# Attention and soft-MoE on one core: the side work of the attention loop in another order

## The chip, the cores and the metric

The kernel runs on one core of a Trainium2 chip. The core has a matrix engine (PE, with PEld for its weight loads), a vector engine (DVE), an activation engine (ACT), a general engine (POOL), and a queue engine that starts most transfers here (SP). Each engine runs its own instructions strictly in the order of its queue, and waits on semaphores for the others. The metric is the device time of one execution in microseconds (us); of several executions the median is given.

## The reference

Block-sparse attention over 4 batches, 8 heads, 768 positions and 64 channels is followed by a soft mixture of experts over the 3072 tokens that it gives.

```python
def _attn_ref(q, k, v):                       # block, window = 32, 16
    k_sum = k.reshape(B, H, nb, block, D).max(axis=3)
    v_sum = v.reshape(B, H, nb, block, D).mean(axis=3)
    scores_l = scale * q @ k^T, kept where abs(i - j) < window
    scores_s = scale * q @ k_sum^T + log(block)
    a = softmax over both kinds of keys together
    return a @ concat(v, v_sum)

def _moe_ref(x, phi, w1, w2):                 # 8 experts, 4 slots each
    logits = x @ phi
    d = softmax of logits over the tokens;  slot_input = d.T @ x
    slot_out[e] = relu(slot_input[e] @ w1[e]) @ w2[e]
    c = softmax of logits over the slots;   return c @ slot_out
```

Only the shape of the computation is kept above; everything is float32.

## The kernel before

The attention is a loop of 24 steps (`NSTEP`). A step is one third of the positions (256 of 768, `tp` = 0, 1, 2) of four heads of one batch (`hb`, 0 to 7; three steps in a row share one `hb` and so one tile `kk` of keys and one tile `q`). The loop is a software pipeline written out by hand: in pass `i` stand the scores and the exponentials of step `i`, the transposes of step `a = i-1`, and the product with the values and the normalisation of step `b = i-2`. The order of the instructions in the program is the order on every engine; no scheduler moves anything.

The parts of a step, with their lines before the change:

- `scores` (L226, PE) multiplies q with the keys, into two PSUM tiles `s` that have one buffer each.
- `soft_max` (L245, DVE) adds the mask and finds the row maxima, four for each of two halves, 0 and 1. `soft_exp` of half 0 (L255, ACT) takes four exponentials with the maxima as bias. For half 1, `soft_sub` (L261, POOL) subtracts the maxima, and `soft_exp` (L257, ACT) is one exponential over the whole half.
- `trans` (L267, PE) transposes the exponentials, and `evac` (L272, ACT) copies them to `ptr`.
- `values` (L283, PE) multiplies with v, and `norm` (L301 to L304, DVE) divides by the sums and writes the tokens `x`.
- For the keys of the next `hb`: `k_max` (L179, DVE) reduces blocks of 32 keys, `k_edge` (L195, POOL) and `k_put` (L202, POOL) lay them beside the keys for the scores.
- `put_v` (L339) writes the sums of the blocks of v into the tile of v that `values` reads.

Beside the steps runs side work, in pieces named by a letter and a number. A piece is a generator: `begin` runs it up to its first `yield`, which is its work on PE into a PSUM bank, and `flush` runs the rest, which empties the bank.

- `V n` (`v_sum`, L319): sums of v over blocks for `hb` n, 96 small matmuls into two banks; then four copies on ACT (L330) and four additions on DVE (L332) into `vsst`.
- `X n` (`route_x`, L350): transposes 128 tokens; then a copy on ACT (L353) to `xt`.
- `L n` (`route_l`, L363): the logits of 512 tokens, from four `xt`; then a running maximum on DVE (L381, L382), exponentials and copies on ACT (L383 to L385), and the running sum on DVE (L389).
- `T n` (`route_t`, L395): transposes the exponentials `dt`; then a copy on DVE (L398) to `dsb`.
- `D n` (`route_d`, L406): adds these tokens, weighted, to the slots; then DVE adds the result to `acc` (L421; L419 for the first).

All pieces take their banks in turn from the two of the pool `ps_p`. In the tail every second one comes from `ps_t` (`tail`), which holds the transposes during the loop.

The table `PLAN` says which pieces stand in which pass, to the left of the bar (`front`) or to its right (`back`); `LOADS` says how many pieces of the expert weights (512 KB each) a pass asks for on SP. The list `room` says which buffers a weight piece may take, and from which pass on; the later ones are buffers of the attention that have been used for the last time. On SP a pass also asks for the tile of v eight steps on, and once in three passes for keys and q. After the loop comes a drain with the last routing, then the first expert matmul over 32 weight pieces (L663), the second one (L696), and the combination of the slots, with the output.

Of the kernel before, what the change touches and what calls it, by code (L numbers as in the profile page):

```python
# [21 lines left out]
NSTEP = HB * TPS  # L22
# [16 lines left out]


PLAN = {
    1: "| V0",
    3: "| V1",
    6: "X0 X1 | V2",
    7: "X2 X3 |",
    8: "X4 X5 | L0",
    9: "T0 | V3",
    10: "| D0",
    12: "X6 X7 | V4",
    13: "| L1",  # L50
    14: "T1 | D1",
    15: "X8 X9 | V5",
    16: "X10 X11 |",
    17: "| L2",
    18: "X12 X13 | V6",
    19: "T2 | D2",
    20: "X14 X15 |",
    21: "X16 X17 | V7",
    22: "| L3",
    23: "T3 | D3",  # L60
    24: "X18 X19 |",
}

LOADS = [0, 0, 1, 1, 1, 1, 1, 1, 1, 1, 1, 1, 1, 1, 1, 1, 1, 1, 2, 1, 4, 2, 1, 3, 4, 1]


BESIDE = "C0 C1 S0 C2 S1 C3 S2 C4 S3 C5 S4 S5"
# [7 lines left out]
def attention_soft_moe(  # L75
# [13 lines left out]
    nc = tc.nc  # L89
# [33 lines left out]
    xflat = [x.rearrange("p t c -> p (t c)") for x in xs]  # L123
# [2 lines left out]
    room = [(t, 0) for t in was] + [(vflat[0], 18), (vflat[1], 19), (vflat[2], 20)]  # L126
    room += [(t, 20) for t in kflat[0] + [qflat[0]]] + [(vflat[3], 21), (vflat[4], 22), (vflat[5], 23)]
    room += [(t, 23) for t in kflat[1] + [qflat[1]] + xflat[0:2]] + [(vflat[6], 24), (vflat[7], 25)]
    room += [(t, 26) for t in xflat[2:]]
    NPRE = len(room)  # L130
    slots_ = [t for t, _ in room]
    now = [0]
# [13 lines left out]
    def load_k(hb, pr=None):  # L146
        if hb < HB:
            k = kk[hb % 2][:, K0:EA0]
            c = slice(0, 2 * KP) if pr is None else slice(KP * pr, KP * pr + KP)
            nc.sync.dma_start(out=k[:, c], in_=kx[hb, :, c])  # L150
# [22 lines left out]
    def k_max(hb, part):  # L173
        if hb >= HB:
            return
        if hb not in kst:
            kst[hb] = wk.tile([128, 2, NB], F32, name="ks", bufs=2)
        pr, th = part // 3, part % 3
        nc.vector.reduce_max(  # L179
            out=kst[hb][:, pr, 8 * th : 8 * th + 8],  # L180
            in_=kview(hb)[:, pr, 16 + 256 * th : 272 + 256 * th].rearrange("p (b k) -> p b k", k=32),
            axis=AX,
        )
# [13 lines left out]
    def k_put(hb, eng):  # L197
        if hb >= HB:
            return
        for c in range(2):  # L200
            o = 0 if c else 32
            eng.tensor_copy(  # L202
                out=eview(hb, c)[:, :, :, o : o + NB], in_=kst[hb].unsqueeze(2).broadcast_to([128, 2, NTT, NB])
            )
# [13 lines left out]
    def scores(i):  # L218
        hb, tp = steps[i]
        s = [ps_s.tile([128, 4, 128], F32, name=f"s{r}") for r in range(2)]  # L220
        for u in range(4):
            tt, pr = u // 2, u % 2
            for r in range(2):
                for c in range(2):
                    o = 128 * tt + 64 * c
                    nc.tensor.matmul(  # L226
                        s[r][64 * c : 64 * c + 64, u, :].rearrange("p (a k) -> p a k", a=2),
                        lhsT=qs[hb % NQR][64 * r : 64 * r + 64, tp, pr, o : o + 64],
                        rhs=keys(hb, r, c, pr, 2 * tp + tt),
                        start=True,  # L230
                        stop=True,
                        tile_position=(64 * r, 64 * c),
                    )
        ps_[i] = s

    def soft_max(i, r):
        hb, tp = steps[i]
        s = ps_[i][r]
        m = wk.tile([128, 4], F32, name="m", bufs=4)
        p = wk.tile([128, 4, 128], F32, name="p", bufs=4)  # L240
        for u in range(4):
            t = 2 * tp + u // 2
            mk = 0 if t == 0 else 2 if t == NTT - 1 else 1

            nc.vector.tensor_tensor_reduce(  # L245
                out=p[:, u, :], in0=s[:, u, :], in1=maskv[:, mk, :], scale=-0.125, scalar=-NEG,
                op0=ALU.add, op1=ALU.min, accum_out=m[:, u : u + 1],
            )
        p_[i, r] = p, m
# [9 lines left out]
    def soft_sub(i, r):  # L259
        p, m = p_[i, r]  # L260
        nc.gpsimd.tensor_tensor(out=p, in0=m.unsqueeze(2).broadcast_to([128, 4, 128]), in1=p, op=ALU.subtract)  # L261
# [8 lines left out]
    def evac(i, r):  # L270
        ptr = wk.tile([128, 4, 128], F32, name="ptr", bufs=4)
        nc.scalar.copy(out=ptr, in_=ptr_[i, r])  # L272
        ptr_[i, r] = ptr
# [62 lines left out]
    def put_v(i, c, eng):  # L336
        n0 = 0 if c else 96
        src = vsst[96 : 96 + NB, i // TPS % 2].rearrange("n h c -> n (h c)").unsqueeze(1)
        eng.tensor_copy(  # L339
            out=vs[i % NV][n0 : n0 + NB, c].rearrange("n t h c -> n t (h c)"), in_=src.broadcast_to([NB, 2, 260])  # L340
        )
# [154 lines left out]
    def flush(gs):  # L496
        for g in gs:
            while advance(g):
                pass
# [3 lines left out]
    def begin(names):  # L503
        gs = [pieces_of[n[0]](int(n[1:])) for n in names.split()]
        for g in gs:
            advance(g)
        return gs
# [31 lines left out]


    held = []
    for i in range(NSTEP + 2):
        a, b = i - 1, i - 2
        front, back = (PLAN.get(i, "|")).split("|")
        hb, tp = i // TPS, i % TPS
        now[0] = i
        if i < NSTEP:
            scores(i)
            soft_max(i, 0)
            soft_exp(i, 0)  # L550
            soft_max(i, 1)
            soft_sub(i, 1)
        if tp == 1:
            for part in range(3):
                k_max(hb + 1, part)
            k_edge(hb + 1, nc.gpsimd)
        if tp == 2:
            for part in range(3, 6):
                k_max(hb + 1, part)
            k_put(hb + 1, nc.gpsimd)  # L560
        if 0 <= a < NSTEP:
            trans(a, 0)
            trans(a, 1)
            evac(a, 0)
            evac(a, 1)
        if i < NSTEP:
            soft_exp(i, 1)
        flush(held)
        held = begin(front)
        if b >= 0:  # L570
            values(b)
            norm(b)
        flush(held)
        held = begin(back)
        if i == 1:
            flush(held)
            for c in range(2):
                put_v(0, c, (nc.gpsimd, nc.vector)[c])
        if 0 <= a < NSTEP:
            if i > 1:  # L580
                for c in range(2):
                    put_v(a, c, nc.gpsimd)
        if tp == 0:
            load_k(hb + 1) if hb else None
            load_q(hb + 1) if hb else None
        if b >= 0:
            load_v(b + NV)
        for _ in range(LOADS[i]):
            load_piece()
    flush(held)  # L590

    tail.append(1)
    now[0] = NSTEP + 2
    gx = begin("X20 X21")
    flush(gx)
    gx = begin("X22 X23")
    gl = begin("L4")
    flush(gx)
    flush(gl)
    gt = begin("T4")  # L600
    gl = begin("L5")
    flush(gt)
    flush(gl)
    gd = begin("D4")
    gt = begin("T5")
    flush(gd)
    R = lanes()
    advance(R)
    flush(gt)
# [227 lines left out]
```

## Time and profile before

| what | us |
|---|---|
| median of 3 executions | 267.58 (267.22 to 270.6) |
| the profiled execution | 267.19 |
| its span, first to last instruction | 265.4 |
| PE busy in the span | 193.6 |
| DVE busy | 130.5 |
| ACT busy | 107.9 |
| POOL busy | 75.9 |

The mean granted PE clock was 0.864. The profile of one execution lists for every instruction when it began and how long it took, and infers from semaphore events what each wait ended on. In a row of the timeline the columns are the start in us, the duration in us, engine, line, operation, tiles, and how many instructions are merged; in brackets stands the idle time of that engine just before, and what ended it. In a row of the waits the columns are the engine and the line that waited, the one it waited for, the sum in us, how often, and the longest. The 40 slices of the page (6.6 us each; busy share in tenths, PEclk the granted clock) show the stages at a glance:

```profile
PE   7397667396477848496887476775776899999970
PEclk9659999979769986669797957979599899999996
DMA  7997999527825954284288120941693989999968
```

### The profile page before, as it was taken

What the parts mean: (1) busy time and instruction counts of PE and PEld (TensorE: products, weight loads), DVE (VectorE), ACT (ScalarE), POOL (GpSimd) and SP (SyncE); (2) the same over time, 40 slices, a digit from 0 to 9 for tenths busy, and PEclk for the clock granted to TensorE, in tenths of its full rate; (3) what the DMA queues carried; (4) which work ended last, traced back from release to release, by engine and by line L of the source; (5) the groups of instructions that cost most, each with busy time, mean ns of one, the idle gap of its engine ahead of it and who ended that gap; (6) DMA issues with size and microseconds to landing.
All of it is one profiled execution on the core that took longest, in us unless ns stands there. A gap on an engine that the chain in (4) does not pass through costs nothing.

```text
span 265.4 us, 8592 instructions
## 1 busy us (share of the span) xinstructions
PE 193.6 (73%) x3473; PEld 144.0 (54%) x3473; DVE 130.5 (49%) x671; ACT 107.9 (41%) x277; POOL 75.9 (29%) x139
## 2 busy tenths in 40 slices
PE   7397667396477848496887476775776899999970
PEld 5385556285365646375766345664463455564550
DVE  2658684446248455335482534536333476503470
ACT  1165665536254552245363505555043012302350
POOL 8345555314335441323252404315100100000000
PEclk9659999979769986669797957979599899999996
DMA  7997999527825954284288120941693989999968
GB/s 253 320 318 213 354 269 352 141 60 232 295 109 173 312 153 142 65 318 144 66 261 313 48 81 0 330 170 64 218 415 96 332 290 418 419 416 415 370 256 326
DMA packets 19384, 63.19 MB, mean 238 GB/s; under 512 B 2320, under 2 KB 2320, under 8 KB 19344
## 3 DMA queue, kind: packets, MB, share of 16 engines
q1 hardware_dynamic: 19200, 62.28, 67.0%
q8 instruction: 27, 0.44, 0.6%
q10 hardware_dynamic: 144, 0.36, 0.4%
q14 instruction: 13, 0.11, 0.1%
HBM read 56.34 MB, written 6.29 MB: 236 GB/s over the span
## 4 chain that ended last, share of the span: by engine, by line
PE 52%; DVE 20%; ACT 9%; POOL 8%; issue 6%; DMA 2%; POOLq 0%; SPq 0%; ACTq 0%; DVEq 0%
DVE p L245 12%; PE s L226 12%; POOL p L261 8%; PE o L283 7%; PE hps L663 6%; PE so L696 6%; PE pp L319 4%; ACT p L257 4%; PE pp L406 3%; PE pp L350 3%; PE op L733 3%; PE pt L267 2%; PE pp L363 2%; DVE x L304 2%; ACT xt L353 2%
## 5 line engine op out<-in xcount | busy, mean ns | idle before, releaser
L255 ACT ACTIVATE p<-p,m 128x128 f32<-128x128 f32 x96 | 30.8, 391 | 82.1 <-DVE m L245 82.1
L245 DVE CUSTOM_DVE_ANT_0 p<-s,cs 128x128 f32<-128x128 f32 x192 | 42.5, 287 | 39.2 <-PE s L226 39.2
L261 POOL TENSOR_TENSOR p<-m,p 128x512 f32<-128x512 f32 x24 | 24.9, 1039 | 100.4 <-DVE m L245 100.4
L226 PE MATMUL s<-kk,q 64*64 64x128 f32 x768 | 36.1, 325 | 7.9 <-POOL kk L202 3.7
L283 PE MATMUL o<-v,ptr 120*64 120x65 f32 (+1 forms) x768 | 33.5, 249 | 7.2 <-issue 5.8
L226 PEld LDWEIGHTS s<-kk,q 64*64 64x64 f32 x768 | 28.4, 163 | 16.5 <-issue 7.1
L283 PEld LDWEIGHTS o<-v,ptr 120*64 120x64 f32 (+1 forms) x768 | 29.6, 160 | 11.8 <-issue 10.2
L267 PE MATMUL pt<-ident,p 128*128 128x128 f32 x192 | 31.2, 313 | 1.4 <-issue 1.4
L339 POOL COPY v<-vsst 24x520 f32<-24x520 f32 x47 | 29.1, 620 | 10.6 <-DVE vsst L332 8.3
L267 PEld LDWEIGHTS pt<-ident,p 128*128 128x128 f32 x192 | 24.7, 161 | 8.2 <-issue 7.7
L272 ACT COPY ptr<-pt 128x512 f32<-128x512 f32 x48 | 25.4, 576 | 6.6 <-PE pt L267 6.4
L350 PE MATMUL pp<-ident,x 128*128 128x128 f32 x88 | 14.5, 306 | 12.7 <-ACT vsst L330 7.4
L301 DVE TENSOR_SCALAR z<-o 128x8 f32<-128x8 f32 x24 | 4.0, 165 | 34.3 <-PE o L283 34.1
L350 PEld LDWEIGHTS pp<-ident,x 128*128 128x128 f32 x88 | 11.6, 159 | 14.2 <-ACT vsst L330 7.8
L179 DVE TENSOR_REDUCE ks<-kk 128x8 f32<-128x256 f32 x48 | 17.1, 412 | 4.4 <-DMA kk<-kx 4.3
L257 ACT ACTIVATE p<-p 128x512 f32<-128x512 f32 x24 | 15.1, 630 | 9.8 <-POOL p L261 9.8
L304 DVE TENSOR_TENSOR x<-o,z 128x256 f32<-128x256 f32 x48 | 18.1, 419 | 0.8
L319 PE MATMUL pp<-v,cs 64*32 64x64 f32 x768 | 12.1, 256 | 6.3 <-ACT xt L353 4.0
L245 DVE DVE_READ_ACCUMULATOR2_ANT m<- 128x1 f32 x192 | 16.1, 84 | 0.0
L353 ACT COPY xt<-pp 128x512 f32<-128x512 f32 x22 | 12.1, 582 | 8.8 <-PE pp L350 7.3
L319 PEld LDWEIGHTS pp<-v,cs 64*32 64x32 f32 x768 | 9.7, 120 | 8.4 <-ACT xt L353 5.2
L406 PE MATMUL pp<-x,dsb 128*32 128x512 f32 (+1 forms) x40 | 7.5, 833 | 7.4 <-DVE dsb L398 5.7
(132 smaller groups left out, 220.6 us busy)
## 6 DMA issues: line engine op xcount, KB each, us to landing
wa<-w SPq DMA_DIRECT2D x34, 512.0 KB, 6.7
v<-w SPq DMA_DIRECT2D x12, 512.0 KB, 5.0
kk<-kx SPq DMA_DIRECT2D x7, 800.0 KB, 7.4
q<-qx SPq DMA_DIRECT2D x7, 768.0 KB, 9.3
v<-va SPq DMA_DIRECT2D x24, 195.0 KB, 5.3
v<-vb SPq DMA_DIRECT2D x24, 195.0 KB, 5.5
kk<-w SPq DMA_DIRECT2D x9, 512.0 KB, 6.3
x<-w SPq DMA_DIRECT2D x6, 512.0 KB, 4.7
```

The costliest lines, as they stand in the source:

```text
L226: nc.tensor.matmul(s[r][64 * c : 64 * c + 64, u, :].rearrange("p (a k) -> p a k", a=2), lhsT=qs[hb % NQR][64 * r : 64 * r + 64, tp, pr, o ...
L245: nc.vector.tensor_tensor_reduce(out=p[:, u, :], in0=s[:, u, :], in1=maskv[:, mk, :], scale=-0.125, scalar=-NEG, op0=ALU.add, op1=ALU.min, ...
L255: nc.scalar.activation(out=p[:, u, :], in_=p[:, u, :], func=AF.Exp, scale=-1.0, bias=m[:, u : u + 1])
L257: nc.scalar.activation(out=p, in_=p, func=AF.Exp)
L261: nc.gpsimd.tensor_tensor(out=p, in0=m.unsqueeze(2).broadcast_to([128, 4, 128]), in1=p, op=ALU.subtract)
L267: nc.tensor.transpose(pt[:, u, :], p[:, u, :], ident)
L272: nc.scalar.copy(out=ptr, in_=ptr_[i, r])
L283: nc.tensor.matmul(o[64 * c : 64 * c + 64, r, u, :], lhsT=ptr[0:K, u, 64 * c : 64 * c + 64], rhs=v[0:K, c, tt, 2 * pr + r, :], start=True, ...
L304: nc.vector.tensor_tensor(out=x[:, r], in0=o[:, r, :, 0:64].rearrange("p (t q) d -> p t q d", t=2), in1=z[:, r].rearrange("p (t q) -> p t ...
L319: nc.tensor.matmul(pv[c][32 * g : 32 * g + 32, 0:64], lhsT=cs[64 * c : 64 * c + 64, o : o + 32], rhs=v[64 * c : 64 * c + 64, c, t % 2, g, ...
L339: eng.tensor_copy(out=vs[i % NV][n0 : n0 + NB, c].rearrange("n t h c -> n t (h c)"), in_=src.broadcast_to([NB, 2, 260]))
L350: nc.tensor.transpose(pv[:, 128 * c : 128 * c + 128], x, ident)
```

## The change

The change touches the table `PLAN`, the table `LOADS`, one line of `room`, the body of the loop, and the drain. What each part does:

- V's sums stand one pass earlier (V0 in pass 0 instead of 1, and so on). The rest of the pieces that stood to the right of the bar is flushed at the head of the next pass, before the maxima, and no longer after the last exponential.
- A piece to the left of the bar is begun and flushed at once, between `evac` and the last exponential; before, it was begun there after that exponential and flushed after `norm`.
- The stages of the routing stand a pass apart or more. X20 to X23, L4, L5, T4 and D4, which stood after the loop, stand in passes 24 to 26; the loop has one pass more.
- `put_v` moves to the head of the pass, and so does `k_put`; both are on POOL, ahead of `soft_sub`. The two copies of `put_v` for step 0 are both on POOL (one was on DVE).
- `k_max` stands in `tp` 0 and 1 instead of 1 and 2. The load of keys and q stands in `tp` 2 for `hb`+2, instead of `tp` 0 for `hb`+1: one pass earlier.
- Weight pieces are asked for in other passes, 37 within the loop instead of 34; two of the buffers of `x` are free one pass later.

```diff
@@ PLAN, some lines
-    1: "| V0",
-    6: "X0 X1 | V2",
-    7: "X2 X3 |",
-    8: "X4 X5 | L0",
-    13: "| L1",
-    14: "T1 | D1",
+    0: "| V0",
+    5: "| V2",
+    6: "X0 X1 |",
+    7: "X2 X3 | L0",
+    8: "T0 | V3",
+    12: "X6 X7 | L1",
+    13: "T1 | D1",
+    14: "X8 X9 | V5",
...
+    24: "X18 X19 | L4",
+    25: "T4 ; X20 X21 | D4",
+    26: "X22 X23 | L5",
@@ LOADS
-LOADS = [0, 0, 1, 1, 1, 1, 1, 1, 1, 1, 1, 1, 1, 1, 1, 1, 1, 1, 2, 1, 4, 2, 1, 3, 4, 1]
+LOADS = [0, 1, 1, 1, 1, 1, 1, 1, 1, 1, 1, 1, 1, 1, 1, 1, 1, 1, 1, 1, 5, 1, 1, 7, 1, 1, 2]
@@ the loop
-    for i in range(NSTEP + 2):
+    for i in range(NSTEP + 3):
...
         if i < NSTEP:
             scores(i)
+        if i == NSTEP + 1:
+            tail.append(1)
+        flush(held)
+        if 0 <= a < NSTEP:
+            for c in range(2):
+                put_v(a, c, nc.gpsimd)
+        if tp == 2:
+            k_put(hb + 1, nc.gpsimd)
+        if i < NSTEP:
             soft_max(i, 0)
             soft_exp(i, 0)
             soft_max(i, 1)
             soft_sub(i, 1)
+        if tp < 2:
+            for part in ((0, 1, 2), (3, 4, 5))[tp]:
+                k_max(hb + 1, part)
         if tp == 1:
-            for part in range(3):
-                k_max(hb + 1, part)
             k_edge(hb + 1, nc.gpsimd)
-        if tp == 2:
-            for part in range(3, 6):
-                k_max(hb + 1, part)
-            k_put(hb + 1, nc.gpsimd)
         if 0 <= a < NSTEP:
             trans(a, 0)
             trans(a, 1)
             evac(a, 0)
             evac(a, 1)
+        for group in front.split(";"):
+            flush(begin(group))
         if i < NSTEP:
             soft_exp(i, 1)
-        flush(held)
-        held = begin(front)
-        if b >= 0:
+        if 0 <= b < NSTEP:
             values(b)
             norm(b)
-        flush(held)
         held = begin(back)
...
-        if tp == 0:
-            load_k(hb + 1) if hb else None
-            load_q(hb + 1) if hb else None
+        if tp == 2:
+            load_k(hb + 2)
+            load_q(hb + 2)
         if b >= 0:
             load_v(b + NV)
         for _ in range(LOADS[i]):
             load_piece()
```

In the orders below the changed kernel's lines are one higher than before (L331 is L330 of before). On ACT, in passes 6 to 9 before, from V2's copies (`vsst`) to the first exponentials of L0 (`dt`), with the copies of X2 to X5 (`xt`) between them:

```order
L330 COPY vsst<-pp 24x64 x4
L353 COPY xt<-pp 128x512 x2
L255 ACTIVATE p<-p,m 128x128 x4
L272 COPY ptr<-pt 128x512 x2
L257 ACTIVATE p<-p 128x512
L353 COPY xt<-pp 128x512 x2
L255 ACTIVATE p<-p,m 128x128 x4
L272 COPY ptr<-pt 128x512 x2
L257 ACTIVATE p<-p 128x512
L378 ACTIVATE dt,stat<-pp,stat 128x128
```

The same stretch on ACT after the change, from V2's copies to L0, in passes 6 to 8; the copies of `xt` are X0 to X3:

```order
L331 COPY vsst<-pp 24x64 x4
L256 ACTIVATE p<-p,m 128x128 x4
L273 COPY ptr<-pt 128x512 x2
L354 COPY xt<-pp 128x512 x2
L258 ACTIVATE p<-p 128x512
L256 ACTIVATE p<-p,m 128x128 x4
L273 COPY ptr<-pt 128x512 x2
L354 COPY xt<-pp 128x512 x2
L258 ACTIVATE p<-p 128x512
L379 ACTIVATE dt,stat<-pp,stat 128x128
```

V2's copies moved from behind the last exponential of pass 7 to ahead of the first ones of pass 6; X's copies moved from behind a pass's last exponential to ahead of it; L0's exponentials moved from behind those of pass 9 to ahead of those of pass 8.

On SP, passes 2 and 3 before: tiles of v (`v_93`, `v_94`), the weight pieces (`wa`), and the keys and q of `hb` 2 (`kk_89`, `q_91`):

```order
L159 DMA v_93<-va 96x520
L160 DMA v_93<-vb 96x520
L142 DMA wa_107<-w 128x1024
L150 DMA kk_89<-kx 128x1600
L154 DMA q_91<-qx 128x1536
L159 DMA v_94<-va 96x520
```

The same on SP after the change, from pass 1 on:

```order
L143 DMA wa_107<-w 128x1024
L151 DMA kk_89<-kx 128x1600
L155 DMA q_91<-qx 128x1536
L160 DMA v_93<-va 96x520
L161 DMA v_93<-vb 96x520
L143 DMA wa_108<-w 128x1024
```

The keys moved past a pair of loads of v, and the first weight piece stands ahead of both.

On POOL, passes 4 to 6 before: the subtractions (`p<-m,p`), the edges of the keys, the sums of blocks of v (`v_96`, `v_97`) and of keys (`kk_89<-ks`):

```order
L261 TENSOR_TENSOR p<-m,p 128x512
L195 COPY kk_89<-kk_89 128x12x16 x4
L339 COPY v_96<-vsst 24x520 x2
L261 TENSOR_TENSOR p<-m,p 128x512
L202 COPY kk_89<-ks 128x12x24 x2
L339 COPY v_97<-vsst 24x520 x2
L261 TENSOR_TENSOR p<-m,p 128x512
```

The same on POOL after the change:

```order
L340 COPY v_96<-vsst 24x520 x2
L262 TENSOR_TENSOR p<-m,p 128x512
L196 COPY kk_89<-kk_89 128x12x16 x4
L340 COPY v_97<-vsst 24x520 x2
L203 COPY kk_89<-ks 128x12x24 x2
L262 TENSOR_TENSOR p<-m,p 128x512
```

The copies into v and those of the keys' sums stand ahead of the pass's subtraction now, and behind it before.

More of the change, by code (lines that the diff above doesn't have):

```diff
@@ L41 @@
 PLAN = {
-    1: "| V0",
-    3: "| V1",
-    6: "X0 X1 | V2",
-    7: "X2 X3 |",
-    8: "X4 X5 | L0",
-    9: "T0 | V3",
-    10: "| D0",
-    12: "X6 X7 | V4",
-    13: "| L1",
-    14: "T1 | D1",
[L52 to L61, printed above, removed]
+    0: "| V0",
+    2: "| V1",
+    5: "| V2",
+    6: "X0 X1 |",
+    7: "X2 X3 | L0",
+    8: "T0 | V3",
+    9: "X4 X5 | D0",
+    11: "| V4",
+    12: "X6 X7 | L1",
+    13: "T1 | D1",
+    14: "X8 X9 | V5",
+    15: "X10 X11 | L2",
+    16: "T2 | D2",
+    17: "| V6",
+    18: "X12 X13 |",
+    19: "X14 X15 | L3",
+    20: "T3 | V7",
+    21: "X16 X17 | D3",
+    24: "X18 X19 | L4",
+    25: "T4 ; X20 X21 | D4",
+    26: "X22 X23 | L5",
 }
-LOADS = [0, 0, 1, 1, 1, 1, 1, 1, 1, 1, 1, 1, 1, 1, 1, 1, 1, 1, 2, 1, 4, 2, 1, 3, 4, 1]
+LOADS = [0, 1, 1, 1, 1, 1, 1, 1, 1, 1, 1, 1, 1, 1, 1, 1, 1, 1, 1, 1, 5, 1, 1, 7, 1, 1, 2]
 BESIDE = "C0 C1 S0 C2 S1 C3 S2 C4 S3 C5 S4 S5"
@@ L128, in attention_soft_moe @@
     room += [(t, 23) for t in kflat[1] + [qflat[1]] + xflat[0:2]] + [(vflat[6], 24), (vflat[7], 25)]
-    room += [(t, 26) for t in xflat[2:]]
+    room += [(t, 26) for t in xflat[2:4]] + [(t, 27) for t in xflat[4:]]
     NPRE = len(room)
@@ L565, in attention_soft_moe @@
             evac(a, 1)
+        for group in front.split(";"):
+            flush(begin(group))
         if i < NSTEP:
             soft_exp(i, 1)
-        flush(held)
-        held = begin(front)
-        if b >= 0:
+        if 0 <= b < NSTEP:
             values(b)
             norm(b)
-        flush(held)
         held = begin(back)
[L575 to L582, printed above, removed]
-        if tp == 0:
-            load_k(hb + 1) if hb else None
-            load_q(hb + 1) if hb else None
+        if tp == 2:
+            load_k(hb + 2)
+            load_q(hb + 2)
         if b >= 0:
@@ L590, in attention_soft_moe @@
     flush(held)
[L592 to L604, printed above, removed]
+    now[0] = NSTEP + 3
     gt = begin("T5")
-    flush(gd)
     R = lanes()
```

## The prediction

> **What bounds the kernel now.** I read the stages first (windows: length; busy us and count of PE, PEld, DVE, ACT, POOL; granted clock; DMA share; GB/s), cut where the first masked maximum (L245) of steps 4 and 23 and the first expert matmul (L663, at 209.7) start.
>
> ```profile
> 29.83 0.29 DVE L245 CUSTOM_DVE_ANT_0 p<-s,cs 128x128 f32<-128x128 f32 x1 [1.02 <-PE s L226]
> 181.34 0.29 DVE L245 CUSTOM_DVE_ANT_0 p<-s,cs 128x128 f32<-128x128 f32 x1 [0.65 <-PE s L226]
> ...
> 11.30:29.80 18.50, 15.03 (x412) 12.64 (x411) 12.64 (x83) 11.49 (x30) 9.32 (x15) 0.79 0.93 296
> 29.80:181.30 151.50, 105.75 (x2172) 86.12 (x2172) 77.73 (x457) 71.58 (x190) 54.39 (x93) 0.84 0.56 187
> 181.30:209.70 28.40, 18.66 (x248) 13.35 (x248) 11.95 (x50) 9.86 (x28) 3.80 (x6) 0.88 0.60 220
> 209.70:265.40 55.70, 46.75 (x600) 26.10 (x600) 23.97 (x73) 13.67 (x28) 0.76 (x1) 0.93 0.92 361
> 23.00:47.50 24.50, 17.86 (x508) 15.07 (x504) 15.73 (x95) 14.24 (x36) 13.37 (x23) 1.00 0.91 300
> 101.80:128.00 26.20, 17.95 (x308) 13.89 (x305) 12.10 (x71) 11.21 (x32) 7.80 (x14) 0.76 0.47 161
> ```
>
> Steps 4 to 22 take 151.5 us, 8.0 each, and in them no engine is full: PE 70%, DVE 51%. So order bounds them. PE's waits say which order; one step, 7, shows it in full.
>
> ```profile
> PE pp L350 <- ACT vsst L330: 7.4, 2, 3.7
> PE pp L395 <- ACT dt L383: 6.2, 3, 3.1
> PE s L226 <- POOL kk L202: 3.7, 4, 1.7
> ...
> 47.56 1.10 PE L226 MATMUL s<-kk,q 64*64 64x128 f32 x32
> 48.60 1.09 PE L267 MATMUL pt<-ident,p 128*128 128x128 f32 x8
> 48.81 0.29 DVE L245 CUSTOM_DVE_ANT_0 p<-s,cs 128x128 f32<-128x128 f32 x1 [3.74 <-PE s L226]
> 49.15 1.28 ACT L255 ACTIVATE p<-p,m 128x128 f32<-128x128 f32 x4 [3.79 <-DVE m L245]
> 50.33 1.04 ACT L272 COPY ptr<-pt 128x512 f32<-128x512 f32 x2
> 50.51 1.07 DVE L179 TENSOR_REDUCE ks<-kk 128x8 f32<-128x256 f32 x3
> 50.76 1.04 POOL L261 TENSOR_TENSOR p<-m,p 128x512 f32<-128x512 f32 x1 [5.67 <-DVE m L245]
> 51.84 0.63 ACT L257 ACTIVATE p<-p 128x512 f32<-128x512 f32 x1 [0.46 <-POOL p L261]
> 52.49 0.88 ACT L330 COPY vsst<-pp 24x64 f32<-24x64 f32 x4
> 52.72 0.99 DVE L332 TENSOR_TENSOR vsst<-pp,vsst 24x64 f32<-24x64 f32 x4 [1.15 <-ACT vsst L330]
> 53.42 1.97 PE L350 MATMUL pp<-ident,x 128*128 128x128 f32 x8 [3.73 <-ACT vsst L330]
> 53.84 1.29 POOL L339 COPY v<-vsst 24x520 f32<-24x520 f32 x2 [0.89 <-DVE vsst L332]
> 55.32 1.68 PE L283 MATMUL o<-v,ptr 120*64 120x65 f32 x32
> 56.94 1.10 PE L226 MATMUL s<-kk,q 64*64 64x128 f32 x32
> 57.08 0.17 DVE L301 TENSOR_SCALAR z<-o 128x8 f32<-128x8 f32 x1 [3.38 <-PE o L283]
> 57.52 0.76 DVE L304 TENSOR_TENSOR x<-o,z 128x256 f32<-128x256 f32 x2
> ```
>
> V2's matmuls were done before 47.56, but their copies (L330) stand on ACT behind this step's last exp (L257), which waits for POOL's subtraction. Both PSUM banks stay taken, PE stands 3.73 us before X2 (L350), then runs it and the values at half clock (1.97, 1.68). The step costs 9.4.
>
> **The change, part by part.** The arithmetic per step is the same; its place moves. Durations still needed, at full clock:
>
> ```profile
> 27.47 1.18 PE L319 MATMUL pp<-v,cs 64*32 64x64 f32 x96
> 41.68 1.04 PE L350 MATMUL pp<-ident,x 128*128 128x128 f32 x8
> 59.87 1.15 PE L283 MATMUL o<-v,ptr 120*64 120x65 f32 x32
> 61.74 1.05 ACT L353 COPY xt<-pp 128x512 f32<-128x512 f32 x2
> 71.16 0.28 DVE L398 COPY dsb<-pp 128x128 f32<-128x128 f32 x1
> 79.71 1.06 PE L406 MATMUL pp<-x,dsb 128*32 128x512 f32 x8 [1.69 <-ACT vsst L330]
> 199.47 1.08 PE L363 MATMUL pp<-xt,cs 128*32 128x128 f32 x32
> 202.22 0.22 DVE L389 SCALAR_TENSOR_TENSOR stat<-stat,st 128x1 f32<-128x1 f32 x1 [1.06 <-ACT st L384]
> 202.31 1.08 PE L363 MATMUL pp<-xt,cs 128*32 128x128 f32 x32
> ```
>
> I count from one step's first L245 to the next one's. The eight maxima take 1.7 (48.81 to 50.51, where L179 follows), k's reductions 1.07, the norm 1.2 (57.08 to 58.28); scores and transposes follow each other after 1.04 (47.56 to 48.60).
>
> *Evacuations at the head.* V's copies and adds now run under the next scores (1.04 on PE). The last exp ends 3.65 after the first maximum (52.46 less 48.81), so in a step whose only side work is V the copies wait 0.6 and the adds push the maxima by 0.7: 1.04+1.04+1.15+1.18 on PE and 0.6 make 5.0. A step without side work is DVE's: 1.7+1.07+1.2=4.0, or PE's 1.04+1.04+1.15 with a hop, 3.3, where k's reductions are over. L's chain (matmul end 200.55 to L389's end 202.44: 1.9) leads the maxima and puts them 0.7 later than scores would.
>
> *X ahead of the last exp, its copies at once.* X, values and then V or L: L waits for the second X copy. Scores 1.04, to the first exp 0.55, exps 1.28, ptr copies 1.05, xt copies 1.05, hops 0.3, L 1.08: 6.3, with the next step's L chain 7.0. V instead of L: 6.6; D (needs the first copy only) 5.8; X alone hides under DVE: 4.2. The later exp is 1.1 later, which the next transposes see only after a step of 4.2.
>
> *Stages a step apart.* T|D: L chain, maxima, k's reductions, dsb 0.28, D 1.06: 6.1 from scores, 5.5 between maxima. T|V: 5.05.
>
> The sum, steps 4 to 22: plain 4, 10: 8.0; plain 22: 3.3; X alone 6, 18: 8.4; V 5, 11, 17: 15.0; X|L 7, 12, 15, 19: 28.0; T|D 13, 16: 11.0; T|V 8, 20: 10.1; X|D 9, 21: 11.6; X|V 14: 6.6. Together 102. To it I add 7: 0.2 a step for hops that the sum leaves out (the 0.46 before L257 is such a one), and 3 for k, next.
>
> *Loads of k one step earlier on SP, its reductions one step earlier too.*
>
> ```profile
> 31.91 1.07 DVE L179 TENSOR_REDUCE ks<-kk 128x8 f32<-128x256 f32 x3 [0.31 <-DMA kk<-kx]
> DMA to landing us min/median/max: 4.6/7.4/7.7
> ```
>
> The load is issued when the scores of a head pair's last step end; the reductions come that step's length plus 1.9 later, 6.2 where it is short (4.3). Against 4.6 to 7.7 that is nothing to 1.5 a pair; for steps 5, 11 and 17 I take 1 each, nearest the median. In return k_put is finished a step before the scores that need it: the 3.7 of L202 go. At the start nothing is won: k(1), whose landing was covered, now holds DVE in step 0, and k(2) passes one pair of v loads (2 x 195 KB, 1.3 us at 296 GB/s) and lands at 30.6 at the latest instead of 31.9. I take 29, as it is also issued up to 3 earlier, behind its scores and not behind a load; the reduction and the norm follow, and step 4's first maximum comes at 29+1.07+1.2=31.3, 1.5 later than 29.83. The w piece of step 1, the bursts of 5 and 7 at steps 20 and 23 queue on SP behind buffers that are free by then; DMA share after 30 us is 0.56, so they are hidden; if they are not, the expert stage waits for its later pieces: 512 KB at 296 GB/s is 1.8 each, and both ends of the range leave room for one.
>
> *put_v ahead of the subtraction on POOL.* Two copies (53.84 to 55.13 in step 7) now run under the maxima, when POOL waits (5.67 before L261). At nothing if maxima cover them; at most 1.3 a step where V's adds are late, and then the last exp has 0.5 to spare: both ends are in the range.
>
> A rule speaks against this move: by the Trainium skill, "SBUF — State Buffer", "Who interferes with whom", some DVE operations and GpSimd's block each other for a whole instruction. By it, if the maxima took the pair, a copy could end up to 1.7 later, the length of the maxima. The page lets an operation with one SBUF input go free, and the maxima read PSUM and one SBUF operand; no row here shows it, and the sum stays.
>
> *Drain.* From step 23's maximum: last exp 3.65; transposes, their copies and X18/X19's 3.35; L4 1.2; to dt 1.3; T4 0.4; X20/21 1.0; values 1.15; norm 1.4; X22/23 with copies 1.8; L5 1.1; then, as now from L5's end (203.39) to 209.70, 6.3. That is 22.7 against 28.4. The expert stage keeps 55.7: all pieces that it starts on have landed, and its DMA stream (share 0.92) starts with it.
>
> 31.3+102+7+22.7+55.7 = 218.7 of span. The profiled execution took 267.19 with a span of 265.4, so 1.8 lies around it: 220.5. The median of the runs shown is 267.58, 0.4 above: **221 us**.
>
> **The rivals.** *PE stays cold.* In 101.8 to 128 the clock was 0.76 with PE standing behind side work; in 23 to 47.5, where PE is 73% busy with short waits, 1.00. My rows are at full clock. Steps 4 to 22 hold 19x3.3 of scores, transposes and values, six V, nine X pairs, four L and four D: 87 us of PE work; were a third of it at half clock, as 0.84 means now, it would cost up to 28: 249. Against it: the waits that precede the slow stretches are those removed. The Trainium skill ("TensorE: Matmul & The Clock Gate", Part 1, the HAM clock gate) says the same of the cause: an idle window of about 3.4 us halves the clock, a busy one restores it. By that rule the sum stands, and the trace agrees (3.73 idle, then 1.97 for 1.04).
>
> *k paces the steps, and DVE stands with it: the slower end.* k's first reduction blocks norm and the next maxima. The denser steps ask more of DMA (300 GB/s at share 0.91 in 23 to 47.5, as it stands). If k lands 11 us after issue, 4.8 x 6 pairs less the 3 counted: 247. It decides against the kernel only if k needs some 15.5 us: (273-221+3)/6=9.2 beyond 6.2. The longest now is 7.7.
>
> *The waits only change places.* Head evacuations hold the maxima as much as the old ones held PE; then only k_put's 3.7 and the drain's 5.7 are won, less 1.5: 260, or within 2% with a few late pieces.
>
> **How the numbers follow.** My forecast 0.80; cold PE 0.07; k at 11 us 0.05, at 15 us 0.03; waits change places 0.05. The low end is the sum without the 7 and with a drain 2 shorter: 212. The high end takes half the cold cost and 1 us for k in the other three pairs: 221+14+3, 238. What lies beyond is about 2 in 10. Two per cent, about what a measurement of this kernel tells from no change, is 262 to 273: faster 0.92, same 0.05, slower 0.03.
>
> **What would show it.** PE's waits on L330 and L383 ahead of L350 and L395 gone; PEclk near 1 from 30 us to the expert stage; step 23's maximum near 140 instead of 181.34; L663 near 163; L202 gone from the waits of the scores; new, small: L179 behind DMA, maxima behind L332 and L389. It is wrong if L179 waits several us in each pair, if X|L steps stay near 9, or if the expert stage stretches beyond 56 because its pieces land late.

## The result, and the profile after

The changed kernel takes 220.56 us (median of 4 runs, 218.82 to 224.13); the kernel before took 269.09 us beside it (267.22 to 271.01). The ratio is 0.8175, with a 95% interval of 0.805 to 0.830: faster. The forecast was 221. The profiled execution took 219.1 us with a span of 217.3. Some executions of a kernel are a few per cent slower than the rest, so all ratios and intervals here (not the medians) leave these out, and none is given where too few others were left.

The stages, cut at the same events as in the prediction: the first masked maximum of steps 4 and 23 and the first expert matmul. The diff adds one line ahead of the kernel's functions, so L245 is now L246, and the first expert matmul has become L647. First the three events in the timeline, then the windows with the same columns as before:

```profile
29.92 0.28 DVE L246 CUSTOM_DVE_ANT_0 p<-s,cs 128x128 f32<-128x128 f32 x1
...
139.88 0.29 DVE L246 CUSTOM_DVE_ANT_0 p<-s,cs 128x128 f32<-128x128 f32 x1
...
160.29 0.66 PE L647 MATMUL hps<-wa,W1ST 128*32 128x256 f32 x4 [0.54 <-DVE rz L479]
...
29.90:139.90 110.00, 91.11 (x2178) 75.35 (x2179) 76.60 (x457) 70.91 (x190) 54.21 (x93) 0.95 0.80 245
139.90:160.30 20.40, 15.83 (x241) 11.38 (x240) 9.59 (x46) 9.28 (x25) 3.62 (x6) 0.98 0.89 326
160.30:217.30 57.00, 48.14 (x600) 26.50 (x600) 23.96 (x73) 13.67 (x28) 0.72 (x1) 0.92 0.91 354
```

| stage | before | predicted | after |
|---|---|---|---|
| to step 4's first maximum | 29.8 | 31.3 | 29.9 |
| steps 4 to 22 | 151.5 | 102 + 7 | 110.0 |
| drain | 28.4 | 22.7 | 20.4 |
| expert stage | 55.7 | 55.7 | 57.0 |

DVE, ACT and POOL are as busy in the steps as before (DVE 76.6 us against 77.7); what went is idle time, and PE's slow clock (0.95 granted against 0.84; its busy time fell from 105.8 to 91.1). Now PE's largest waits, in the view of waits (total, times, longest):

```profile
PE s L227 <- issue: 7.1, 3, 3.2
PE o L284 <- issue: 4.8, 3, 2.2
PE s L227 <- DVE m L246: 3.1, 2, 2.7
PE pp L407 <- DVE z L302: 2.3, 2, 1.4
PE s L227 <- DVE kk L203: 2.0, 1, 2.0
PE pp L320 <- issue: 1.7, 1, 1.7
```

The waits for V's copies and L's exp ahead of X and T (7.4 and 6.2) are gone from the head of the list. On top stands something that the prediction never spoke of: three lines of "issue", waits that end with nothing that the profile shows, 13.6 us in seven of them. Step 11 has the longest; its timeline:

```profile
67.49 0.34 SPq L151 DMA_DIRECT2D kk<-kx  x1
67.87 0.53 SPq L155 DMA_DIRECT2D q<-qx  x1
67.92 1.15 PE L284 MATMUL o<-v,ptr 120*64 120x65 f32 x32
...
69.00 1.18 PE L320 MATMUL pp<-v,cs 64*32 64x64 f32 x96
...
73.39 1.36 PE L227 MATMUL s<-kk,q 64*64 64x128 f32 x32 [3.21 <-issue]
...
74.69 1.97 PE L268 MATMUL pt<-ident,p 128*128 128x128 f32 x8
```

Values and V run back to back, then PE stands 3.21 us before the scores, whose inputs were there (POOL's copies into `kk`, the last of them, ended at 69.96), and the transposes behind them run at half clock (1.97 for 1.04). The trace's DMA records tell what came just ahead. Queue q8 carries PE's own instructions, 27 packets of 16 KB in the whole execution:

```profile
q8 instruction: 27, 0.44, 0.9%
```

I set each packet beside the place in PE's program where it is first needed. These places lie 256 PE instructions apart (matmuls, weight loads and the semaphore instructions between them; PE's 7055 records make 27.6 such blocks). All seven waits, then six of the blocks without one; the first column is when PE passed the place before, the third how busy the 16 DMA engines were from then until the packet started (worked out from the records):

```
PE passes   packet          DMA busy   PE passes     of it
a place     start   end     between    next place    waiting
 24.37      28.83   30.23    1.0         31.73        0.85
 31.73      35.34   36.55    1.0         37.90        1.73
 37.90      41.75   42.82    1.0         44.09        1.74
 54.42      58.29   59.55    1.0         61.23        2.19
 67.98      71.07   72.02    0.85        73.39        3.21
 91.96      96.97   98.09    0.93        99.66        0.91
107.16     109.98  111.02    0.90       112.50        2.94
 61.23      62.33   63.52    0.29        67.98        none
122.34     122.73  123.75    0.0        128.34       none
128.34     128.41  129.45    0.0        131.63        none
 20.82      21.36   22.55    1.0         24.37        none
 50.19      51.34   52.80    1.0         54.42        none
 73.39      77.67   78.88    1.0         80.53        none
```

In the two rows with idle DMA engines the packet starts within 0.4 us of PE's passing; in the seven with a wait the engines are nearly full and it starts 2.8 to 5.0 later. Full engines make a packet late often and not always: in two of the last three rows it starts 0.5 and 1.2 later. Nor is a late packet enough for a wait: in the last row it comes 4.3 late, and PE, in part at half clock there, takes 7.1 us for the block. PE goes on 1.3 to 1.7 after the packet's end in each of the seven. So, as an estimate from these rows, a block can be run some 2.5 us after it is asked for at best and 5 to 8 in the seven cases, and PE is through with the 256 before it sooner where V's 192, which take 1.2 us, stand among them. The Trainium skill ("Runtime: NRT & Kernel Launch", Instruction fetch mechanics) describes blocks of 16 KiB, 256 instructions, fetched by the sequencer's own DMA queue. The packets here agree. It also calls the cost mostly hidden, which the 13.6 us here contradict.

### The profile page after: what moved, and what is told of

Same layout as the page of the kernel before. It is cut to its first block, busy times and chain, and to the rows that moved or that the text cites. A ratio compares the mean times of both kernels' runs of the same rounds, so it can differ in the third digit from the quotient of the medians.

```text
span 217.3 us, 8616 instructions
## 1 busy us (share of the span) xinstructions
PE 178.3 (82%) x3473; PEld 132.1 (61%) x3473; DVE 128.4 (59%) x670; ACT 107.4 (49%) x277; POOL 76.6 (35%) x140
## 3 DMA queue, kind: packets, MB, share of 16 engines
HBM read 56.34 MB, written 6.29 MB: 288 GB/s over the span
## 4 chain that ended last, share of the span: by engine, by line
PE 53%; DVE 13%; ACT 10%; issue 8%; POOL 7%; DMA 6%; SPq 0%; POOLq 0%; ACTq 0%
PE hps L647 8%; PE so L680 7%; PE s L227 7%; PE pt L268 6%; PE o L284 6%; DVE p L246 5%; DMA kk<-kx 3%; PE op L717 3%; POOL p L262 3%; PE pp L351 3%; PE pp L407 3%; DMA q<-qx 3%; ACT xt L354 3%; ACT ptr L273 2%; PE pp L320 2%
## 5 line engine op out<-in xcount | busy, mean ns | idle before, releaser
L256 ACT ACTIVATE p<-p,m 128x128 f32<-128x128 f32 x96 | 30.7, 390 | 34.7 <-DVE m L246 34.7
L246 DVE CUSTOM_DVE_ANT_0 p<-s,cs 128x128 f32<-128x128 f32 x192 | 42.5, 286 | 8.8 <-PE s L227 8.3
L227 PE MATMUL s<-kk,q 64*64 64x128 f32 x768 | 30.1, 282 | 12.1 <-issue 7.1
L227 PEld LDWEIGHTS s<-kk,q 64*64 64x64 f32 x768 | 23.1, 136 | 19.0 <-issue 13.6
L284 PE MATMUL o<-v,ptr 120*64 120x65 f32 (+1 forms) x768 | 29.8, 232 | 4.8 <-issue 4.8
L284 PEld LDWEIGHTS o<-v,ptr 120*64 120x64 f32 (+1 forms) x768 | 26.0, 144 | 9.5 <-issue 9.2
L268 PE MATMUL pt<-ident,p 128*128 128x128 f32 x192 | 29.9, 300 | 1.1 <-ACT p L258 0.9
L268 PEld LDWEIGHTS pt<-ident,p 128*128 128x128 f32 x192 | 22.6, 151 | 6.7 <-issue 3.2
L258 ACT ACTIVATE p<-p 128x512 f32<-128x512 f32 x24 | 15.3, 639 | 9.0 <-POOL p L262 9.0
L246 DVE DVE_READ_ACCUMULATOR2_ANT m<- 128x1 f32 x192 | 15.9, 83 | 0.0
L351 PE MATMUL pp<-ident,x 128*128 128x128 f32 x88 | 13.1, 296 | 0.0
L320 PE MATMUL pp<-v,cs 64*32 64x64 f32 x768 | 10.5, 235 | 2.3 <-issue 1.7
L333 DVE TENSOR_TENSOR vsst<-pp,vsst 24x64 f32<-24x64 f32 x32 | 7.2, 224 | 7.3 <-ACT vsst L331 6.5
L647 PE MATMUL hps<-wa,W1ST 128*32 128x256 f32 x136 | 10.9, 468 | 0.5 <-DVE rz L479 0.5
```

What stands on the lines that cost most here:

```text
L227: nc.tensor.matmul(s[r][64 * c : 64 * c + 64, u, :].rearrange("p (a k) -> p a k", a=2), lhsT=qs[hb % NQR][64 * r : 64 * r + 64, tp, pr, o ...
L246: nc.vector.tensor_tensor_reduce(out=p[:, u, :], in0=s[:, u, :], in1=maskv[:, mk, :], scale=-0.125, scalar=-NEG, op0=ALU.add, op1=ALU.min, ...
L256: nc.scalar.activation(out=p[:, u, :], in_=p[:, u, :], func=AF.Exp, scale=-1.0, bias=m[:, u : u + 1])
L268: nc.tensor.transpose(pt[:, u, :], p[:, u, :], ident)
L284: nc.tensor.matmul(o[64 * c : 64 * c + 64, r, u, :], lhsT=ptr[0:K, u, 64 * c : 64 * c + 64], rhs=v[0:K, c, tt, 2 * pr + r, :], start=True, ...
L351: nc.tensor.transpose(pv[:, 128 * c : 128 * c + 128], x, ident)
```

## Experiments: one part alone, or one part undone

In the table: the median; the ratio to the kernel before with its 95% interval (– where none is given); then of the profiled execution the first maximum of step 4, steps 4 to 22, the drain, and, as "instr", the sum of PE's waits for instructions ahead of step 23's maximum: idle time above 0.3 us that ends at the first instruction of a block, 1.2 to 1.7 us after its packet, with the weight loads that run meanwhile taken off (so 13.5 for the 13.6 above). I count them by place and packet and not by the label "issue", because the view of waits names the semaphore event that came last. In u_k it shows

```profile
PE s L227 <- DMA v<-vb: 3.0, 1, 3.0
```

although the scores read no v; this wait too stands at the first instruction of a block and ends 1.3 us after its packet (2.3 us of it count).

| kernel | median us | ratio | to step 4 | steps 4–22 | drain | instr |
|---|---|---|---|---|---|---|
| before | 269.1 | 1 | 29.8 | 151.5 | 28.4 | 8.1 |
| changed | 220.6 | 0.818 (0.805–0.830) | 29.9 | 110.0 | 20.4 | 13.5 |
| b_head | 228.9 | 0.857 (0.841–0.873) | 32.1 | 116.4 | 22.4 | 10.0 |
| u_x | 229.7 | 0.858 (0.841–0.876) | 30.4 | 118.3 | 20.4 | 10.8 |
| u_k | 215.3 | 0.806 (0.794–0.819) | 31.5 | 105.4 | 21.3 | 8.1 |
| u_drain | 220.0 | 0.825 (0.814–0.835) | 30.7 | 113.0 | 21.0 | 13.2 |
| u_drain2 | 221.1 | – | 31.4 | 111.1 | 22.0 | 13.8 |
| e_light | 219.3 | 0.819 (0.813–0.825) | 29.8 | 107.2 | 21.3 | 11.7 |
| e_lk | 213.6 | 0.790 (0.782–0.798) | 29.0 | 106.1 | 21.2 | 7.9 |
| e_v2 | 210.3 | 0.774 (0.768–0.780) | 30.6 | 101.3 | 21.5 | 1.5 |
| e_v2k | 210.5 | 0.788 (0.780–0.796) | 27.6 | 102.5 | 20.7 | 1.9 |
| e_v2l | 209.3 | – | 30.9 | 98.8 | 20.7 | 1.5 |
| c_v2lk | 207.8 | 0.779 (0.774–0.785) | 27.7 | 99.6 | 20.7 | 0.0 |
| e_shift | 224.1 | 0.825 (0.818–0.832) | 38.2 | 110.1 | 20.6 | 15.3 |

**b_head: the evacuations at the head, alone, in the kernel before.**

```diff
             scores(i)
+        flush(held)
+        if i < NSTEP:
             soft_max(i, 0)
...
             soft_exp(i, 1)
-        flush(held)
         held = begin(front)
```

> The kernel before with one line moved: the copies, sums and maxima left over from the step behind (V, L, T, D) are evacuated right behind the scores instead of behind the last exp. Theory (these evacuations held the PSUM banks and are most of the gain): the waits of PE on L330 and L383 go, six V steps and four L steps lose about 3 each, 30 of the 48 us: about 238. Rival (the waits only change places, onto the maxima and k): no more than 10 won, 257 or above.

228.9: more than the theory gave. Moving one flush is worth 40 of the 48.5 us; everything else in the change adds 8. PE's waits in this kernel:

```profile
PE pp L319 <- ACT xt L353: 7.3, 10, 1.5
PE pp L406 <- DVE dsb L398: 6.6, 4, 2.2
PE o L283 <- issue: 4.0, 3, 3.0
```

PE no longer waits for V's copies and L's exponentials ahead of X and T. The largest waits left are those for X's and T's own evacuations (L353, L398) behind the last exp, which the rest of the change moves. The clock follows: 0.97 granted in steps 4 to 22 against 0.84.

**u_x: X and T behind the last exp again.**

```diff
-        for group in front.split(";"):
-            flush(begin(group))
         if i < NSTEP:
             soft_exp(i, 1)
+            held = begin(front)
         if 0 <= b < NSTEP:
             values(b)
             norm(b)
+        if i < NSTEP:
+            flush(held)
```

> The changed kernel with one part undone: the X pieces' copies follow the last exp again and not the copies of ptr. Theory: in the five steps with X and then L or V the copies start at the last exp's end, about 1 us later each, and X with D half of that; 3 to 8 us longer, about 225. Rival (X ahead of the last exp carries much of the gain, since PE stands behind the copies): 15 or more, 236 or above.

229.7, between the two, and the intervals of 0.841 to 0.876 and 0.805 to 0.830 do not meet: X and T ahead are worth about 9. My expectation counted only the steps with X; T rides in the same place. With a step named by its pieces left and right of the bar, T|V in step 8 takes 5.92 for 4.93, T|D in 13 and 16 6.33 for 5.23, X|D in 21 6.32 for 5.45: about 1 in most steps with front work. The waits name both:

```profile
PE pp L407 <- DVE dsb L399: 4.8, 3, 2.4
PE pp L364 <- ACT xt L354: 4.0, 3, 1.4
```

**u_k: k's reductions, copies and loads where they stood.**

```diff
-        if tp == 2:
-            k_put(hb + 1, nc.gpsimd)
...
-        if tp < 2:
-            for part in ((0, 1, 2), (3, 4, 5))[tp]:
-                k_max(hb + 1, part)
         if tp == 1:
+            for part in range(3):
+                k_max(hb + 1, part)
             k_edge(hb + 1, nc.gpsimd)
+        if tp == 2:
+            for part in range(3, 6):
+                k_max(hb + 1, part)
+            k_put(hb + 1, nc.gpsimd)
...
-        if tp == 2:
-            load_k(hb + 2)
-            load_q(hb + 2)
+        if tp == 0 and hb:
+            load_k(hb + 1)
+            load_q(hb + 1)
```

> The changed kernel with one part undone: k's reductions, POOL's edge and block copies and the loads of k and q for the next head pair stand where they stood before. Theory: the scores of a pair's first step wait for POOL's block copies again (3.7 in all before, up to 1.7 a pair where the step is short), 4 to 8 us longer: 225 to 229. Rival (k costs the changed kernel as much as it won, as the 3 us counted for it say): within 2 us of 220.6.

Neither: 215.3, so undoing this part seems to win (the intervals overlap). In the profiled executions the waits for instructions fell from 13.5 to 8.1. The changed kernel issues k and q, 800 and 768 KB a pair, at the end of the steps in which six of the eight V pieces start (2, 5, 8, 11, 14, 17), as in step 11 above. Whether the gain lies in these waits is what e_lk and e_v2k ask below.

**u_drain, u_drain2: the last routing stages after the loop again.** X20 to X23, L4, L5, T4 and D4 go back from PLAN's rows 24 to 26 into the hand-written sequence behind the loop. u_drain leaves out the addition of D4 to `acc`; u_drain2 has it.

```diff
-    24: "X18 X19 | L4",
-    25: "T4 ; X20 X21 | D4",
-    26: "X22 X23 | L5",
+    24: "X18 X19 |",
...
-    for i in range(NSTEP + 3):
+    for i in range(NSTEP + 2):
```

> The changed kernel with one part undone: X20 to X23, L4, L5, T4 and D4 follow the loop one after another again. Theory: the drain from step 23's first maximum to the first expert matmul goes from 20.7 back to about 28.4, the steps stay: 227 to 229. Rival (the drain became shorter only because the steps ahead of it left less behind): 221 to 223.

> The changed kernel with X20 to X23, L4, L5, T4 and D4 after the loop as before, with all of its sums (u_drain leaves out the addition of D4 to the sums in acc). Theory, after u_drain: the drain of about 20 us is not due to these pieces' places, 219 to 222, and the drain from step 23's first maximum to the first expert matmul is within 2 us of 20.7. Rival (the new places save 5 or more in the drain): 225 or above.

220.0 and 221.1, with drains of 21.0 and 22.0 against 20.4: these places are worth at most 1.6 us. b_head's drain of 22.4 tells where most of the 8 came from: the moved flush, which stands in the last passes too.

## Experiments: the waits for instructions

**e_light: fewer transfers early.**

```diff
-LOADS = [0, 1, 1, 1, 1, 1, 1, 1, 1, 1, 1, 1, 1, 1, 1, 1, 1, 1, 1, 1, 5, 1, 1, 7, 1, 1, 2]
+LOADS = [0, 0, 0, 0, 0, 0, 0, 0, 0, 0, 0, 0, 2, 2, 2, 2, 2, 2, 3, 4, 5, 1, 1, 7, 1, 1, 2]
```

> The changed kernel with its weight pieces at other steps: none in steps 0 to 11, two a step in 12 to 17, three and four in 18 and 19, the rest as it was. The changed kernel stood 10 us in steps 3 to 11 where PE waits for nothing but its own instructions; each of these waits ends 1.3 to 1.7 us after a 16 KB packet of the instruction queue has landed, and the packet starts up to 5 us after PE has crossed the place in its program that asks for it. Theory A (the packet queues behind the data transfers): in steps 3 to 11 the packets start within 1 us and the waits fall from 10 to under 3; in 12 to 19 they stay or grow. Rival B (V's 192 instructions in 1.2 us outrun the packets whatever the transfers do): the same waits at the same places, 8 us or more in steps 3 to 11. The whole: 214 to 219 by A, 220 to 222 by B.

Between the two. In steps 3 to 11 the waits are 0.5, 1.35, 0.96 and 3.15 (step 11), 6.0 together at places where there were 9.7. Packets still start up to 4 us late there, since k, q and v are loading too, so A's "within 1 us" and "under 3" fail; B's "8 or more" fails as well. In 12 to 19 there are 5.7, where there were 3.8. The time, 219.3, is hardly less: weight pieces are only a part of what the packets wait behind.

**e_v2: the same block sums in half the matmuls.**

```diff
-                for g in range(4):
+            for g in range(2):
+                for c in range(2):
...
-                        pv[c][32 * g : 32 * g + 32, 0:64],
+                        pv[c][r : r + 32, 0:128].rearrange("p (h d) -> p h d", h=2),
...
-                        rhs=v[64 * c : 64 * c + 64, c, t % 2, g, 0:64],
+                        rhs=v[64 * c : 64 * c + 64, c, t % 2, 2 * g : 2 * g + 2, 0:64],
```

> The changed kernel with V's block sums in 24 matmuls of 128 columns instead of 48 of 64, its copies and sums two each instead of four; the same sums. PE then runs 96 instructions fewer in each of eight V pieces, for 0.4 us more each. By theory B the waits for instructions go nearly all (13.6 to under 4) and the time falls to about 213; by A they fall by less than half, since the packets start as late as before, and the time is 216 to 221.

210.3, better than B's 213. Of the 13.5 us of waits 1.5 are left, and the instruction packets fall from 27 to 24, as 8 x 96 instructions in blocks of 256 should:

```profile
37.19 1.51 PE L321 MATMUL pp<-v,cs 64*32 64x128 f32 x48
...
q8 instruction: 24, 0.39, 0.8%
```

V takes 1.51 now instead of 1.18 and still the steps are 8.7 shorter. Packets still come late: one asked for at 74.28 starts at 79.63, and PE does not wait for it. So both halves are needed for a wait: a late packet (A) and 256 instructions in a hurry (B). Removing the hurry is the one that pays. The edit also halves V's copies and additions, and no run has that alone. Steps 8, 17 and 20, which had no wait for instructions, are 0.3 shorter each (step 17: 4.62 for 4.93); six such steps make some 2 of the 10 us, by estimate.

**e_lk, e_v2k, e_v2l, c_v2lk: the edits combined.** e_lk is e_light with u_k's edit; e_v2k and e_v2l are e_v2 with u_k's edit and with e_light's LOADS; c_v2lk has all three.

> e_light with k's reductions, POOL's edge and block copies and the loads of k and q where they stood before, as in u_k. u_k was 5 us faster than the changed kernel. Theory A (its gain is that the transfers fall at other times against the instruction packets): with the transfers light, e_lk and e_light differ by less than 2 us. Rival (k's new place itself costs about 5): e_lk is 4 us or more under e_light.

> e_v2 with k's reductions, POOL's copies and the loads of k and q where they stood before (the edit of u_k). In e_v2 only 1.5 us of waits for instructions are left, so that k's place shows alone. Theory (u_k won its 5 us because its transfers met the instruction packets at other times; taken without these waits its profiled span is 5 us above the changed kernel's): e_v2k is within 2 us of e_v2's 210.3, or up to 5 slower. Rival (k's new place itself costs about 5): 206 or below.

> e_v2 with the weight pieces at the steps of e_light. With the waits for instructions gone already, theory says that the light steps win nothing more there: within 2 us of 210.3; at most 1 us from a faster start. Rival (the light steps win by themselves, since loads of k and v land sooner): 207 or below.

> All three edits together: V in half the matmuls, light first steps, k at its place of before. If the three were independent gains (10, 1 and 5 us): about 205. By the theory (all three shorten the same waits for instructions, which V's edit removes alone): 208 to 212.

e_lk contradicts theory A as I had put it: k's place won 5.7 although the early transfers were lighter. They were not light enough to test it, as e_light showed (7.9 us of waits are left against 11.7). With V's instructions halved k's place wins nothing: 210.5 against 210.3, and by the ratio it rather loses. If its new place cost 5 us by itself, it would do so there too. So its cost in the changed kernel lies, as far as these runs tell, in the waits for instructions, though e_lk's 5.7 is more than the 3.8 by which its waits fell. (The 5 us between the spans in e_v2k's expectation do not come out of the two profiles: 214.1 less 8.1 is 206.0 for u_k, 217.3 less 13.5 is 203.8 for the changed kernel, 2.2 apart.) Why the old place makes fewer of them stays open: that k and q are issued where V starts fits step 11 of the changed kernel, but u_k still waits 2.3 there, and e_lk 4.4 in step 18. The light steps are worth 1 more, within what the runs can tell. c_v2lk is the lowest median, 207.8, at the lower edge of the theory's 208 to 212, with no wait for instructions above 0.3 us, and 12.8 below the changed kernel; by the ratio (0.774 and 0.779) it is not told from e_v2, so V's edit is what carries it. Both beat the changed kernel. c_v2lk's steps 4 to 22, drain and expert stage:

```profile
27.67:127.27 99.60, 90.29 (x1894) 73.36 (x1893) 74.88 (x447) 68.99 (x179) 54.45 (x94) 1.00 0.84 283
127.27:147.94 20.67, 15.91 (x239) 11.38 (x238) 9.69 (x46) 9.40 (x25) 3.62 (x6) 1.00 0.85 323
147.94:204.46 56.52, 46.81 (x600) 26.07 (x600) 24.08 (x73) 13.67 (x28) 0.74 (x1) 0.92 0.91 357
```

The clock is 1.00 throughout the steps, PE is 91% busy, and the DMA share is not lower than in the changed kernel (0.84 against 0.80): it was not the amount of the transfers that held the steps up.

**e_shift: the same program, its blocks cut elsewhere.**

```diff
+    for _ in range(32):
+        nc.tensor.matmul(wm[:, 0:8], lhsT=acc[:, 0:128], rhs=acc[:, 0:8], start=True, stop=True)
     load_k(0, 0)
```

> The changed kernel with 32 more warm-up matmuls of 8 columns ahead of the loop, 128 PE instructions with their weight loads, in a stretch where PE waits for the first data. Nothing in the loop differs; only where the program's blocks of 256 instructions begin. Theory (one packet carries 256 instructions; a wait arises where PE runs through 256 faster than a packet asked for at their start arrives, 3.5 to 6 us): the waits move. Worked out from the changed kernel's trace with its waits taken out, the fastest blocks end after 2.5 us at V2's matmuls (step 5) and after 2.1 us at the scores behind V3 (about 55 us), so waits of 1 to 4 us come there; the blocks that ended at the scores of steps 11 and 18 (3.2 and 2.9 us of wait) now end elsewhere, after 4.4 us and more, so these two waits shrink to under 1. The total stays: 218 to 224, waits of 8 to 15 us in the same view. Rival (V pieces and scores make PE wait by themselves, wherever the blocks begin): the waits of steps 11 and 18 stay at the same matmuls.

```profile
PE o L284 <- issue: 5.8, 3, 2.6
PE s L227 <- issue: 5.3, 3, 4.0
PE pp L320 <- issue: 4.2, 1, 4.2
...
q8 instruction: 28, 0.46, 0.8%
```

The waits moved, and their sum stayed about as it was (15.3 for 13.5, just above the range). V2's matmuls in step 5 now wait 4.2, where a wait was worked out; step 11's 3.2 is gone. Two forecasts missed: the scores behind V3 waited only 0.3, as their packet started 0.4 us after it was asked for, and the wait of step 18 went to matmuls 128 instructions further on without shrinking (4.0; its packet started 6.2 late). So the place follows the blocks; the size follows how late the packet starts, and that differed by 5.8 us between these two though the DMA engines were nearly full ahead of both (0.84 and 0.94). The whole time cannot be compared: the added matmuls took 10.6 us where I had thought PE idle, so step 0 began 9 us later, part of which the loop regained.

## Why the prediction came out right

- **Evacuations at the head.** Right, and most of the gain: b_head alone gives 40 us. The prediction did not divide the gain among the parts; my later expectation for this one, 30, was too low.
- **The sum of the steps.** 102 was worked out; kernels with under 2 us of waits for instructions need 98.8 to 102.5 (their V is 0.3 longer on PE). By step type, predicted, changed kernel, c_v2lk: plain 10: 4.0, 3.78, 3.78; T|D 16: 5.5, 5.24, 5.23; V 17: 5.0, 4.93, 4.90; X|D 21: 5.8, 5.45, 5.45; X|L 15: 7.0, 7.15, 6.29; X alone 18: 4.2, 9.59, 4.21. The excess in single steps of the changed kernel is the waits for instructions, and behind two of them the half clock: step 18 is 5.4 longer than c_v2lk's, 2.94 of it a wait. X|L was taken 0.7 too long: L's chain does not add to the next maximum's time.
- **The allowance of 7: right in size, wrong in content.** "0.2 a step for hops that the sum leaves out" and "3 for k" did not come: the reductions waited 6.6 us for k in all, 3.9 and 2.0 of it ahead of step 1, which leaves the 0.72 at 42.49. What filled it was a wait that I had no term for, although the kernel before already had 8.1 us of it; its view of waits names the larger part (first row below). The forecast is that close because two errors of this step met.

The rows of the kernel before (the first) and of the changed kernel for this and the next point:

```profile
PE o L283 <- issue: 5.8, 2, 3.4
...
DVE ks L180 <- DMA kk<-kx: 6.6, 3, 3.9
...
27.83 1.07 DVE L180 TENSOR_REDUCE ks<-kk 128x8 f32<-128x256 f32 x3
...
42.49 1.07 DVE L180 TENSOR_REDUCE ks<-kk 128x8 f32<-128x256 f32 x3 [0.72 <-DMA kk<-kx]
```

- **The start.** Predicted 1.5 later, measured the same: k(2) was reduced at 27.83, straight behind step 3's maxima, and not at 29.
- **k one step earlier.** "Nothing to 1.5 a pair" for late loads was right (0.7 in all), but its cost was elsewhere, in the waits for instructions: u_k shows 5 us (with overlapping intervals), e_lk 5.7, and e_v2k, where these waits are gone, nothing.
- **put_v ahead of the subtraction.** At nothing, as taken: the subtraction still waits for the maxima alone, and the copies are as long as before (615 ns after, 620 before), so the rule on DVE and GpSimd of the Trainium skill ("SBUF — State Buffer", Who interferes with whom) has no effect to be seen here.

```profile
L340 POOL COPY v<-vsst 24x520 f32<-24x520 f32 x48 | 29.5, 615 | 5.8 <-DVE vsst L333 3.1
L262 POOL TENSOR_TENSOR p<-m,p 128x512 f32<-128x512 f32 x24 | 24.9, 1038 | 61.4 <-DVE m L246 60.5 <-PE pp L351 0.9
```

- **Drain.** 22.7 against 20.4: the shortening was right and a little too small; the two drain kernels show that the new places of X20 to X23, L4, L5, T4 and D4 bring at most 1.6 of the 8.
- **Expert stage.** 55.7 against 57.0, beyond the 56 at which the prediction would see late pieces. The pieces are not late: PE's waits in the stage are as short as before. The whole difference arises in the first expert matmul, whose early part stays longer at half clock; the same 40 matmuls in the kernel before and in the changed one:

```profile
213.11 2.54 PE L663 MATMUL hps<-wa,W1ST 128*32 128x256 f32 x40
163.98 3.58 PE L647 MATMUL hps<-wa,W1ST 128*32 128x256 f32 x40
```

- **The sum.** Luck had a part in it: the start and the drain were taken 1.4 and 2.3 too long, the steps and the expert stage 1.0 and 1.3 too short, and that comes to 1.4 of the span of 217.3.
- **The rivals.** Cold PE: 0.95 granted, and what is missing follows the waits of 3.21 and 2.94. The waits only change places: b_head's 228.9 rules it out. k as the pace: 0.7 us.

## What to carry to other kernels

Free the PSUM banks ahead of the vector work that holds their readers up, and check it alone: one moved flush was 40 of 48 us here. When PE becomes dense, look at its waits that end with "issue" and set them beside the instruction queue's packets: many small matmuls in a row beside full DMA queues make PE wait for its own program, and fewer, wider matmuls can win although each takes longer. A sum that lands on the measured time is not yet explained: here an allowance for one thing was filled by another.

## What the runs showed of the hardware

- PE's instructions come in 16 KB packets of 256, in a queue that the profile counts on the same 16 DMA engines as the data. With the engines nearly idle (share under 0.2) a packet starts 0.1 to 0.9 us after PE's passing a block's end, and 1.1 to 2.1 after it right behind a wait for the packet before (e_light: PE passes at 31.25, the packet starts at 32.96, share 0.02). With full ones it starts anywhere from at once to 6.4 us after it (e_v2l: 107.70 to 114.10). It mostly takes 0.9 to 1.4 us, and a waiting PE goes on 1.2 to 1.7 us later. Waits of 0.3 to 4.4 us follow where PE gets through a block sooner.
- The waits move with the block's cut (e_shift) and go with V's instruction count (e_v2: 13.5 to 1.5 us).
- In the changed kernel waits of 2.94 and 3.21 us halved the clock (transposes at 1.97 us for 1.04), and behind those of 1.74 and 2.19 the next scores ran at full speed. The length alone does not decide it: in u_drain2 a wait of 2.02 did it and one of 2.87 did not, each shown with the next scores. All of these are shorter than the 3.4 us that the prediction quotes.

```profile
45.22 1.02 PE L282 MATMUL o<-v,ptr 128*64 128x65 f32 x21 [2.02 <-issue]
46.17 1.99 PE L225 MATMUL s<-kk,q 64*64 64x128 f32 x32
...
64.02 0.34 PE L282 MATMUL o<-v,ptr 120*64 120x65 f32 x4 [2.87 <-issue]
...
65.28 1.10 PE L225 MATMUL s<-kk,q 64*64 64x128 f32 x32
```
